# Attention over channels followed by a gated feed-forward layer: contiguous loads, scores kept in PSUM, and one written order of emission

## The chip, the cores and the metric

The kernel runs on one core of one Trainium2 chip. The metric is the device time of one execution in microseconds. Three runs of the kernel before gave 912.92, 912.98 and 914.06 us, median 912.98.

Five engines share the work, each with an instruction queue of its own that it runs in order: TensorE (PE) multiplies matrices and writes to PSUM, VectorE (DVE) and ScalarE (ACT) move and transform data, GpSimd (POOL) issues the loads that also convert f32 to bf16, and SyncE (SP) issues the stores. An engine that reaches an instruction whose inputs aren't ready waits, and everything behind it in that queue waits too.

## What is computed

```python
B, N, C = (4, 6016, 256);  d_ff = 1536
# attention over channels, for each of the 4 batches
qn = q / (norm(q, axis=1) + 1e-06)          # norms run over the 6016 rows
kn = k / (norm(k, axis=1) + 1e-06)
s  = kn.transpose(0, 2, 1) @ qn / tau       # 256 x 256 for each batch, tau = 1
a  = softmax(s, axis=-1)                    # sum + 1e-09 in the division
x  = (v @ a).reshape(24064, 256)
# gated feed-forward layer
out = (sigmoid(x @ w_gate) * (x @ w_val)) @ w_out
```

Since `x = v @ a`, both kernels form G = a @ w_gate and H = a @ w_val once for each batch (256 x 1536 each) and then compute sigmoid(v @ G) * (v @ H), so that x itself is never built. The softmax of batch b + 1 has to be complete before the first rows of that batch can go through the feed-forward part.

## The kernel before

**Tiling.** The 6016 rows of a batch are 47 tiles of 128 rows, taken in 12 groups of four (the last has three). Loads of q and k go by such groups, and the feed-forward part goes by the same groups as chunks of 512 rows (384 at the end). Row `t * 128 + p` lies on partition p, so a group is four pieces of 256 numbers on each partition.

**Attention, one group** (`attn_pair_compute`, L119). DVE squares q and k and adds the squares to running sums `acc_q` and `acc_k` (L132, L140, L146). PE multiplies k by q for the group, each half of the 256 x 256 scores in a PSUM tile of its own, `ps_sa` and `ps_sb` (L161). DVE adds both to `s_acc` in SBUF (L169, L171).

**Attention, the end** (`attn_finish`). PE sums the squares over partitions (`ps_nq`, `ps_nk`), ACT takes the roots, DVE inverts them (L193, L196) and scales the scores (L232), finds each row's maximum, ACT takes the exponential with the row sum, and DVE divides (L261). PE transposes the result (L272), and from it and the two weights makes G and H, six blocks of 512 columns each, in `ps_gh`, two matmuls a block (L292), which ACT copies to SBUF as bf16 (L299). The PSUM tiles `ps_sa`, `ps_sb`, `ps_gh`, `ps_nk`, `ps_at` and the transposes of v share two one-buffer pools, `psa` and `pst`.

**Feed-forward, one chunk** (`ffn_gv`, `ffn_out`). PE transposes the chunk of v (`ps_tp`, L322) and DVE copies it to `vT` (L328). For each of 12 blocks f of 128 hidden units PE makes `ps_gate` (L334) and `ps_val` (L343), two matmuls of 512 columns each; ACT takes the sigmoid (L351), DVE multiplies (L356) into `hT`. Two PSUM buffers each for gate and val mean that block f + 2 can't start before ACT and DVE are through with block f. Then 12 matmuls of 256 columns for each tile of rows make the output (`ps_o`, L370), which DVE copies out (L377) and SP stores.

**Order.** The code emits attention of batch 0, and then for each chunk its gate and val part, one or two groups of the next batch's attention (the next batch is spread over chunks 0 to 8, `attn_finish` in chunk 8), and the output matmuls of the chunk before. This is not the order on the engines: a scheduler reorders what is emitted, engine by engine, by priority and by what it takes to be ready. The three weights are loaded first, then q and k.

## Time and profile before

| | |
|---|---|
| median of three runs | 912.98 us |
| span of the profiled execution | 911.6 us, 14333 instructions |
| PE busy | 850.5 us, 93% |
| DVE busy | 652.5 us, 72% |
| ACT busy | 385.6 us, 42% |
| POOL busy | 110.3 us, 12% |
| loads of q, k, v and weights (q0) | 39.33 MB written, 33.1% of the 16 DMA engines |

The profile is one execution, taken by the hardware profiler. A row of its timeline reads: start in us, length in us, engine, line, operation, output and inputs, shape, count, and in brackets how long the engine had been idle before and what released it. A row of its windows reads: stretch, length, then for each engine busy time and number of instructions, then the granted PE clock, the mean number of busy DMA engines as a share of 16 (packets may overlap), and the GB/s moved as written to the destination. Matmuls are pipelined: a row's length includes the time in which the next has begun, so rates are read from the starts of rows.

### The profile page before, as it was taken

The numbers are of one execution on the slowest core, as the hardware profiler recorded it, in microseconds if no ns is written. First come the engines' busy times: TensorE is split into PE (matmuls) and PEld (weight loads), VectorE is DVE, ScalarE is ACT, GpSimd is POOL, SyncE is SP. The second block draws the span as 40 slices with busy tenths as digits, with TensorE's granted clock in tenths as the row PEclk, the third lists the DMA queues.
The fourth block names the chain that finished last, engine by engine and source line by source line (L and its number), as shares of the span: only waits on it lengthen the run. The fifth ranks groups of instructions, "written<-read, shape, count | busy, mean of one in ns | idle before, by whom it ended". The sixth has DMA issues, their size and how long they took to land.

```text
span 911.6 us, 14333 instructions
## 1 busy us (share of the span) xinstructions
PE 850.5 (93%) x5421; PEld 519.5 (57%) x5472; DVE 652.5 (72%) x1162; ACT 385.6 (42%) x660; POOL 110.3 (12%) x153
## 2 busy tenths in 40 slices
PE   1639999999899999999999999999999999999998
PEld 0324556656556565665546556656655656656566
DVE  2989976666998766766899676676747666666664
ACT  0016443345453534434563353443565344353542
POOL 5452000001510000000430000000000000000000
PEclk9999999999999999999999999999999999999999
DMA  9999211321993122113892311311122221221201
GB/s 170 196 150 176 47 37 35 63 43 38 193 144 81 19 54 52 36 36 67 127 205 45 64 36 36 68 38 36 33 58 47 54 47 36 62 44 39 52 24 65
DMA packets 101494, 64.90 MB, mean 71 GB/s; under 512 B 3120, under 2 KB 100912, under 8 KB 101424
## 3 DMA queue, kind: packets, MB, share of 16 engines
q0 software_dynamic: 76592, 39.33, 33.1%
q1 hardware_dynamic: 24832, 24.64, 8.5%
q8 instruction: 43, 0.70, 0.3%
q14 instruction: 27, 0.22, 0.1%
HBM read 78.64 MB, written 24.64 MB: 113 GB/s over the span
## 4 chain that ended last, share of the span: by engine, by line
PE 85%; DVE 6%; DMA 5%; POOL 2%; issue 1%; ACT 1%; POOLq 0%; ACTq 0%
PE ps_val L343 27%; PE ps_gate L334 26%; PE ps_o L370 24%; DMA k_full<-in_k_dram 3%; PE ps_tp L322 2%; PE ps_sb L161 2%; DVE sq L140 2%; DMA q_full<-in_q_dram 2%; PE ps_sa L161 1%; PE ps_gh L292 1%; POOL q_full L113 1%; DVE acc_q L146 1%; DVE acc_k L146 1%; DVE s_acc L171 1%; POOL k_full L117 1%
## 5 line engine op out<-in xcount | busy, mean ns | idle before, releaser
L351 ACT ACTIVATE g_sb<-ps_gate 128x512 bf16<-128x512 f32 (+1 forms) x576 | 334.9, 588 | 413.4 <-PE ps_sa L161 164.6
L356 DVE TENSOR_TENSOR hT<-ps_val,g_sb 128x512 bf16<-128x512 f32 (+1 forms) x576 | 387.6, 680 | 116.4 <-ACT g_sb L351 109.9
L343 PE MATMUL ps_val<-vT,gh_H 128*128 128x512 bf16 (+1 forms) x1150 | 336.9, 374 | 2.2
L334 PE MATMUL ps_gate<-vT,gh_G 128*128 128x512 bf16 (+1 forms) x1107 | 328.3, 375 | 5.1 <-DVE vT L328 4.6
L370 PE MATMUL ps_o<-w_out_sb,hT 128*128 128x256 bf16 x2256 | 273.4, 273 | 4.6 <-DVE out_sb L377 4.6
L370 PEld LDWEIGHTS <-hT 128*128 128x128 bf16 x2256 | 219.4, 98 | 40.7 <-issue 5.3
L343 PEld LDWEIGHTS <-gh_H 128*128 128x128 bf16 x1152 | 112.5, 98 | 128.9 <-issue 1.9
L334 PEld LDWEIGHTS <-gh_G 128*128 128x128 bf16 x1152 | 109.1, 98 | 133.9 <-DVE vT L328 10.3
L377 DVE COPY out_sb<-ps_o 128x256 f32<-128x256 f32 x188 | 79.3, 423 | 106.6 <-PE ps_o L370 105.1
L314 POOL DMA_DIRECT2D v_sb<-in_v_dram x48 | 35.8, 745 | 649.2 <-PE ps_tp L322 576.1
L161 PEld LDWEIGHTS <-k_full 128*128 128x128 bf16 x376 | 39.2, 108 | 49.8 <-DMA k_full<-in_k_dram 25.2
L161 PE MATMUL ps_sa<-q_full,k_full 128*128 128x256 bf16 x188 | 33.9, 307 | 30.3 <-DMA k_full<-in_k_dram 20.7
L113 POOL DMA_DIRECT2D q_full<-in_q_dram x48 | 36.3, 757 | 57.3 <-PE ps_sb L161 21.8
L117 POOL DMA_DIRECT2D k_full<-in_k_dram x48 | 36.5, 759 | 25.3 <-DMA k_full<-in_k_dram 21.7
L161 PE MATMUL ps_sb<-q_full,k_full 128*128 128x256 bf16 x188 | 34.4, 309 | 0.0
L328 DVE COPY vT<-ps_tp 128x1024 bf16<-128x1024 bf16 (+1 forms) x48 | 32.6, 679 | 2.5 <-PE ps_tp L322 1.8
L140 DVE TENSOR_TENSOR sq<-k_full 128x1024 bf16<-128x1024 bf16 (+1 forms) x44 | 29.7, 675 | 2.6 <-DMA k_full<-in_k_dram 2.5
L140 DVE TENSOR_TENSOR sq<-q_full 128x1024 bf16<-128x1024 bf16 (+1 forms) x44 | 29.7, 675 | 1.0 <-DMA q_full<-in_q_dram 1.0
L146 DVE TENSOR_TENSOR acc_q<-acc_q,sq 128x1024 bf16<-128x1024 bf16 (+1 forms) x44 | 29.7, 674 | 0.0
L146 DVE TENSOR_TENSOR acc_k<-acc_k,sq 128x1024 bf16<-128x1024 bf16 (+1 forms) x44 | 29.7, 674 | 0.0
L322 PE MATMUL ps_tp<-ident_bf,v_sb 128*128 128x128 bf16 x376 | 29.3, 219 | 0.1
L322 PEld LDWEIGHTS <-v_sb 128*128 128x128 bf16 x376 | 25.2, 98 | 3.2 <-issue 0.8
(48 smaller groups left out, 180.1 us busy)
## 6 DMA issues: line engine op xcount, KB each, us to landing
out_dram<-out_sb SPq DMA_DIRECT2D x44, 512.0 KB, 3.0
q_full<-in_q_dram POOLq DMA_DIRECT2D x44, 256.0 KB, 10.4
k_full<-in_k_dram POOLq DMA_DIRECT2D x44, 256.0 KB, 10.7
v_sb<-in_v_dram POOLq DMA_DIRECT2D x44, 256.0 KB, 5.2
out_dram<-out_sb SPq DMA_DIRECT2D x4, 384.0 KB, 2.6
w_gate_sb<-in_moe_w_gate_dram POOLq DMA_DIRECT2D x1, 768.0 KB, 6.7
w_val_sb<-in_moe_w_val_dram POOLq DMA_DIRECT2D x1, 768.0 KB, 9.2
w_out_sb<-in_moe_w_out_dram POOLq DMA_DIRECT2D x1, 768.0 KB, 12.5
```

The source lines that it names most:

```text
L113: nc.gpsimd.dma_start(out=st["q_full"][:, t0 : t0 + nt, :], in_=q[ab, t0 * P : (t0 + nt) * P, :].rearrange("(t p) c -> p t c", p=P),)
L117: nc.gpsimd.dma_start(out=st["k_full"][:, t0 : t0 + nt, :], in_=k[ab, t0 * P : (t0 + nt) * P, :].rearrange("(t p) c -> p t c", p=P),)
L140: nc.vector.tensor_tensor(out=sq[:, :nt, :], in0=src[:, t0 : t0 + nt, :], in1=src[:, t0 : t0 + nt, :], op=ALU.mult,)
L146: nc.vector.tensor_tensor(out=acc_t[:, :nt, :], in0=acc_t[:, :nt, :], in1=sq[:, :nt, :], op=ALU.add,)
L161: nc.tensor.matmul(ps_s, lhsT=k_full[:, t, ds(iblk * P, P)], rhs=q_full[:, t, :], start=(u == 0), stop=(u == nt - 1),)
L322: nc.tensor.transpose(out=ps_tp[:, cb, ds(u * P, P)], in_=v_sb[:, u, ds(cb * P, P)], identity=ident_bf,)
L334: nc.tensor.matmul(ps_gate[:, :nrows], lhsT=G_sb[:, ib, ds(f * P, P)], rhs=vT[:, ib, :nrows], start=(ib == 0), stop=(ib == CB - 1),)
L343: nc.tensor.matmul(ps_val[:, :nrows], lhsT=H_sb[:, ib, ds(f * P, P)], rhs=vT[:, ib, :nrows], start=(ib == 0), stop=(ib == CB - 1),)
L351: nc.scalar.activation(out=g_sb[:, :nrows], in_=ps_gate[:, :nrows], func=ACT.Sigmoid,)
L356: nc.vector.tensor_tensor(out=hT[:, f, :nrows], in0=ps_val[:, :nrows], in1=g_sb[:, :nrows], op=ALU.mult,)
L370: nc.tensor.matmul(ps_o, lhsT=hT[:, f, ds(s * P, P)], rhs=w_out_sb[:, f, :], start=(f == 0), stop=(f == FC - 1),)
L377: nc.vector.tensor_copy(out=out_sb[:, s, :], in_=ps_o)
```

## The change

The kernel is written anew around an order of emission that the engines keep: `tc.manual_schedule()` turns the reordering off.

- **Rows.** Partition p now holds rows p * 47 to p * 47 + 46 of a batch (`rows`, `out_rows`), so that a group of four tiles is one contiguous piece of 1024 numbers on each partition, in the loads and in the store. The sums over rows don't depend on which row lies where.
- **Scores.** They are kept transposed (q on the output's partitions, k along its columns), and all 47 tiles accumulate in one PSUM tile `ps_s`. `s_acc` and the DVE additions to it are gone.
- **Norms.** The norm of k is summed with a matrix of ones as before; the norm of q is made as a column, with the squares as weights and one column of ones. In batch 0 the squares go to PE group by group (`norm_mms`) and aren't added up on DVE; DVE squares q and ACT squares k. In the other batches DVE squares and adds as before.
- **Softmax.** The exponential takes a constant shift of -1 / tau in place of the row maximum, and writes bf16 in the layout that the G and H matmuls take, so the transposes are gone. Row sums are four matmuls with one column (`sums`). The division is applied where G and H are moved to SBUF (`gh`), by ACT and DVE in turn.
- **Order.** A block f of gate and val, its evictions, then four output matmuls of the chunk before, then side work out of a table (`side_work`, by slots, where slot = chunk x 12 + f): loads, score matmuls of the next batch, squares, transposes. Chunks 9 and 10 of batches 0 to 2 are "blocks": there the output matmuls stand together behind the 12 gate and val blocks, and the next batch's norms and softmax are placed in them. G and H of the next batch are made in chunk 11.
- **Loads.** All of batch 0's q and k stand ahead of the weights.

```diff
+    def rows(x, b):
+        return x[b].rearrange("(p t) c -> p t c", p=P)
+    pss = pool("pss", 1, space=PSUM)
+    psm = pool("psm", 1, space=PSUM)
+    ctx.enter_context(tc.manual_schedule())
...
+    def load_qk(b, g):
+        t0, nt = groups[g]
+        tiles = []
+        for name, src in (("q", q), ("k", k)):
+            tl = qkpool.tile([P, TPC, C], BF16, tag=name, name=name + "_sb")
+            nc.gpsimd.dma_start(out=tl[:, :nt, :], in_=rows(src, b)[:, t0 : t0 + nt, :])
+            tiles.append(tl)
+        qk[b, g] = tiles
...
+    for g in range(2):
+        load_qk(0, g)
...
+    for g in range(2, NCH):
+        load_qk(0, g)
...
+    nc.gpsimd.dma_start(out=w_gate_sb, in_=moe_w_gate.rearrange("(t p) f -> p t f", p=P))
+    load_v(0, 0)
+    nc.gpsimd.dma_start(out=w_val_sb, in_=moe_w_val.rearrange("(t p) f -> p t f", p=P))
+    load_v(0, 1)
+    nc.gpsimd.dma_start(out=w_out_sb, in_=moe_w_out.rearrange("(t p) c -> p t c", p=P))
...
+    def score(b, g, u):
+        t0, nt = groups[g]
+        q_sb, k_sb = qk[b, g]
+        if g == 0 and u == 0:
+            st[b] = {"s": pss.tile([P, CB, C], FP32, tag="s", name="ps_s")}
+        ps_s = st[b]["s"]
+        t = t0 + u
+        for j in range(CB):
+            mm(
+                ps_s[:, j, :],
+                q_sb[:, u, ds(j * P, P)],
+                k_sb[:, u, :],
+                start=(t == 0 and j == 0),
+                stop=(t == NT - 1),
+                skip_group_check=True,
+            )
...
+    def norm_mms(nq, nk, sq_q, sq_k, nt, first, last):
+        for u in range(nt):
+            mm(nk, ones_bf, sq_k[:, u, :], start=(first and u == 0), stop=(last and u == nt - 1))
+        for u in range(nt):
+            for j in range(CB):
+                mm(
+                    nq[:, j : j + 1],
+                    sq_q[:, u, ds(j * P, P)],
+                    ones_bf[:, 0:1],
+                    start=(first and u == 0 and j == 0),
+                    stop=(last and u == nt - 1),
+                    skip_group_check=True,
+                )
...
+    def norms_mm(b):
+        s = st[b]
+        nq = psm.tile([P, CB], FP32, tag="m", name="ps_nq")
+        acc_q, acc_k = s["acc"]
+        nk = pso.tile([P, C], FP32, tag="o", name="ps_nk")
+        norm_mms(nq, nk, acc_q, acc_k, TPC, True, True)
+        s["nq"], s["nk"] = nq, nk
...
+    def norms_inv(b):
+        s = st[b]
+        for r in (s["rk"], s["rq"]):
+            nc.vector.tensor_scalar(out=r, in0=r, scalar1=1e-6, scalar2=None, op0=ALU.add)
+            nc.vector.reciprocal(r, r)
...
+    def exps(b):
+        s = st[b]
+        s["e"] = attp.tile([P, CB, C], BF16, tag="e", name="e_sb", bufs=2)
+        for j in range(CB):
+            nc.scalar.activation(
+                out=s["e"][:, j, :],
+                in_=s["x"][:, j, :],
+                func=ACT.Exp,
+                bias=shift,
+                scale=s["rq"][:, j : j + 1],
+            )
...
+        ps = (pl or psm).tile([P, FG], FP32, tag=tag or "m", name="ps_gh")
+        for j in range(CB):
+            mm(
+                ps,
+                s["e"][:, j, ds(i * P, P)],
+                w_sb[:, j, ds(fg * FG, FG)],
+                start=(j == 0),
+                stop=(j == CB - 1),
+            )
+        dst = s["gh"][w][:, i, ds(fg * FG, FG)]
+        r = s["rrow"][:, i : i + 1]
+        if n % 2 == 0:
+            nc.scalar.activation(out=dst, in_=ps, func=ACT.Copy, scale=r)
+        else:
+            nc.vector.tensor_scalar(out=dst, in0=ps, scalar1=r, scalar2=None, op0=ALU.mult)
...
+    for g in range(NCH + 1):
+        if g < NCH:
+            sq[g] = (squares(0, g, 0, nc.vector), squares(0, g, 1, nc.scalar))
+            for u in range(groups[g][1]):
+                score(0, g, u)
+        if g >= 1:
+            norm_mms(nq0, nk0, *sq.pop(g - 1), groups[g - 1][1], g == 1, g == NCH)
+    st[0]["nq"], st[0]["nk"] = nq0, nk0
+    norms_sqrt(0)
+    norms_inv(0)
+    scale_k(0)
+    exps(0)
+    sums(0)
+    transpose_v(0, 0)
+    for n in range(len(gh_order)):
+        gh(0, n, *((psg, "g"), (psv, "v"))[n % 2])
...
+        for ci in range(NCH):
+            nb, nci = (b, ci + 1) if ci + 1 < NCH else (b + 1, 0)
+            lb, lci = (b, ci + 2) if ci + 2 < NCH else (b + 1, ci + 2 - NCH)
+            if nb < B:
+                at(ci * FC + 8, transpose_v, nb, nci)
+            if lb < B:
+                at(ci * FC + 0, load_v, lb, lci)
+        n = b + 1
+        if n == B:
+            return side
+        last = 9 * FC
+        for g, (t0, nt) in enumerate(groups):
+            s0 = g * last // NCH
+            at(max(0, s0 - 20), load_qk, n, g)
+            for u in range(nt):
+                at((t0 + u) * last // NT, score, n, g, u)
+            if g == 0:
+                at(0, acc_start, n)
+            for i, (fn, w) in enumerate(((acc_square, 0), (acc_add, 0), (acc_square, 1), (acc_add, 1))):
+                at(s0 + 1 + 2 * i, fn, n, g, w)
+        at(9 * FC + 10, norms_mm, n)
+        at(9 * FC + 11, norms_sqrt, n)
+        at(10 * FC + 1, norms_inv, n)
+        at(10 * FC + 4, scale_k, n)
+        at(10 * FC + 11, exps, n)
+        at(11 * FC + 0, sums, n)
+        for i in range(len(gh_order)):
+            at(11 * FC + i, gh, n, i)
...
+        side = side_work(b)
+        for ci in range(NCH):
+            block = b + 1 < B and ci in (9, 10)
+            for f in range(FC):
+                glu(b, ci, f)
+                flush()
+                if prev is not None and not block:
+                    out_mms(*prev, f * TPC, (f + 1) * TPC)
+                for fn, a in side.get((ci, f), ()):
+                    fn(*a)
+            if prev is not None and block:
+                for s in range(TPC):
+                    out_mms(*prev, s * FC, (s + 1) * FC)
+                    flush()
+            prev = (b, ci)
```

The order of the instructions shows the change at three places.

The first is POOL's queue at the start of the program, where the loads are issued; before, it begins so, with the identity matrix, the three weights, and then q and k in groups:

```order
masks.py:197 MEMSET ident_bf 128x128
L82 DMA w_gate_sb<-in_moe_w_gate_dram 128x2x1536
masks.py:199 ISA
masks.py:199 AFFINE_SELECT ident_bf<-ident_bf 128x128
L86 DMA w_val_sb<-in_moe_w_val_dram 128x2x1536
L90 DMA w_out_sb<-in_moe_w_out_dram 128x12x256
L113 DMA q_full<-in_q_dram 128x4x256
L117 DMA k_full<-in_k_dram 128x4x256
```

Of the change, POOL's queue from the last loads of batch 0's q and k (the two of 768 columns) to the first ones of batch 1:

```order
L95 DMA q_sb<-in_q_dram 128x768
L95 DMA k_sb<-in_k_dram 128x768
L123 DMA w_gate_sb<-in_moe_w_gate_dram 128x2x1536
L104 DMA v_sb<-in_v_dram 128x1024
L125 DMA w_val_sb<-in_moe_w_val_dram 128x2x1536
L104 DMA v_sb<-in_v_dram 128x1024
L127 DMA w_out_sb<-in_moe_w_out_dram 128x12x256
L104 DMA v_sb<-in_v_dram 128x1024
L95 DMA q_sb<-in_q_dram 128x1024
L95 DMA k_sb<-in_k_dram 128x1024
```

The weights moved from ahead of batch 0's 24 loads of q and k to behind them, with three loads of v among and behind them, and batch 1's first q and k stand behind all of these.

The second place is PE's queue where the feed-forward part of batch 0 begins. Before, the first gate matmuls stand behind score matmuls of batch 1:

```order
L161 LDWEIGHTS k_full
L161 MATMUL ps_sa<-q_full,k_full 128x256
L334 LDWEIGHTS gh_G
L334 MATMUL ps_gate<-vT,gh_G 128x512
L334 LDWEIGHTS gh_G
L334 MATMUL ps_gate<-vT,gh_G 128x512
L343 LDWEIGHTS gh_H
L343 MATMUL ps_val<-vT,gh_H 128x512
```

Of the change, the end of the first block (f = 0) of batch 0's first chunk, and the start of the second; all matmuls have the line of a helper, and `ps_s` are batch 1's scores:

```order
L85 LDWEIGHTS gh_H
L85 MATMUL ps_val<-vT,gh_H 128x512
L85 LDWEIGHTS q_sb
L85 MATMUL ps_s<-k_sb,q_sb 128x256
L85 LDWEIGHTS q_sb
L85 MATMUL ps_s<-k_sb,q_sb 128x256
L85 LDWEIGHTS gh_G
L85 MATMUL ps_gate<-vT,gh_G 128x512
```

The score matmuls now come one tile at a time between the blocks of gate and val, the first of them behind the very first block, and the second block stands behind them.

The third place is DVE's queue where the next batch's norms are inverted, in chunk 8 before and in chunk 10 now. Before:

```order
L356 TENSOR_TENSOR hT<-ps_val,g_sb 128x512 x12
L171 TENSOR_TENSOR s_acc<-s_acc,ps_sb 128x256
L377 COPY out_sb<-ps_o 128x256
L193 TENSOR_SCALAR hq_rep<-hq_rep 128x256
L196 RECIPROCAL hq_rep<-hq_rep 128x256
L220 TENSOR_SCALAR gk<-ps_kc 128x2
L232 TENSOR_TENSOR x_sb<-s_acc,hq_rep 128x256
```

Of the change:

```order
L352 COPY out_sb<-ps_o 128x256 x4
L326 TENSOR_TENSOR hT<-ps_val,g_sb 128x512 x2
L216 TENSOR_SCALAR rk<-rk 128x256
L217 RECIPROCAL rk<-rk 128x256
L216 TENSOR_SCALAR rq<-rq 128x2
L217 RECIPROCAL rq<-rq 128x2
L326 TENSOR_TENSOR hT<-ps_val,g_sb 128x512 x3
L227 TENSOR_TENSOR x_sb<-ps_s,rk 128x256 x2
L326 TENSOR_TENSOR hT<-ps_val,g_sb 128x512 x4
```

The inversion stood behind all twelve products `hT` of a chunk, among the copies of finished output; it now stands between the second and the third product of a chunk, and the scaling of the scores between the fifth and the sixth.

More of the change, by code (lines that the diff above doesn't have):

```diff
@@ L2 @@
-import math
 from contextlib import ExitStack
@@ L321, in ffn_gv, with transpose_v @@
+    vts = {}
+    def transpose_v(b, ci):
+        t0, nt = groups[ci]
+        v_sb = vs.pop((b, ci))
+        ps_tp = psm.tile([P, CB, CH], BF16, tag="m", name="ps_tp")
+        for u in range(nt):
             for cb in range(CB):
```

483 lines of the change are left out of this document (161 added, 322 removed).

## The prediction

> **What bounds the kernel now.** First the page: span, share of PE, the span in 40 slices, the chain that ended last.
>
> ```profile
> span 911.6 us, 14333 instructions
> PE 850.5 (93%) x5421; PEld 519.5 (57%) x5472; DVE 652.5 (72%) x1162; ACT 385.6 (42%) x660; POOL 110.3 (12%) x153
> PE   1639999999899999999999999999999999999998
> PEclk9999999999999999999999999999999999999999
> PE 85%; DVE 6%; DMA 5%; POOL 2%; issue 1%; ACT 1%; POOLq 0%; ACTq 0%
> ```
>
> A slice is 22.8 us. PE is full from the fifth on, and nearly idle in the first three. So there are two questions: how soon PE can begin, and how close to its own work it runs afterwards. For the second, PE's rates from its timeline and the chain:
>
> ```profile
> 643.49 0.59 PE L334 MATMUL ps_gate<-vT,gh_G 128*128 128x512 bf16 x2
> 650.39 0.59 PE L334 MATMUL ps_gate<-vT,gh_G 128*128 128x512 bf16 x2
> 120.81 4.80 PE ps_o L370 x44
> 245.20 0.61 PE L322 MATMUL ps_tp<-ident_bf,v_sb 128*128 128x128 bf16 x8
> 245.65 0.60 PE L161 MATMUL ps_sa<-q_full,k_full 128*128 128x256 bf16 x4
> 80.12 0.59 PE L334 MATMUL ps_gate<-vT,gh_G 128*128 128x512 bf16 x2 [0.32 <-DVE vT L328]
> 899.04 8.42 PE ps_o L370 x77
> ```
>
> Eight blocks (two gate and two val matmuls each) take 650.39 - 643.49 = 6.90 us, so 0.2156 a matmul of 512 columns; 44 output matmuls of 256 columns take 4.80, so 0.1091; eight transposes take 0.45, so 0.056. For 384 columns I take three quarters of 512, 0.162. The feed-forward part begins at 80.1 and PE ends at 899.04 + 8.42 = 907.5; the last copy, store and landing end the span 4.1 later. Work between, in these rates: gate and val 4 x (11 x 48 x 0.2156 + 48 x 0.162) = 486.4; output 188 x 12 x 0.1091 = 246.1; transposes 20.7; scores of three batches 282 x 0.1091 = 30.8, less 0.9 that was done by 80.1; G and H of three batches 72 x 0.2156 = 15.5; norms, transposes and columns in `attn_finish` about 4.6. Sum 803. The stretch is 827.4, so **24 us are waits**, 8 in each of the first three batches. Some are seen:
>
> ```profile
> 231.50 2.78 PE L370 MATMUL ps_o<-w_out_sb,hT 128*128 128x256 bf16 x24 [1.56 <-DVE out_sb L377]
> 247.48 0.38 PE L334 MATMUL ps_gate<-vT,gh_G 128*128 128x512 bf16 x1 [1.24 <-DVE vT L328]
> 777.77 0.74 POOL L314 DMA_DIRECT2D v_sb<-in_v_dram  x1 [15.39 <-PE ps_tp L322]
> 793.90 0.74 POOL L314 DMA_DIRECT2D v_sb<-in_v_dram  x1 [15.39 <-PE ps_tp L322]
> ```
>
> In the last batch, which has no side work, a chunk takes 16.13 (793.90 - 777.77) for 48 x 0.2156 + 48 x 0.1091 + 0.45 = 16.03 of work: 0.1 of wait a chunk. There is little to win there.
>
> For the first question, the start:
>
> ```profile
> 0.00:4.00 4.00, 0.00 (x0) 0.00 (x0) 0.17 (x2) 1.28 (x1) 3.04 (x9) 1.00 0.29 28
> 4.00:8.00 4.00, 0.00 (x0) 0.00 (x0) 0.00 (x0) 0.00 (x0) 3.93 (x6) 1.00 1.06 204
> 24.00:28.00 4.00, 3.25 (x16) 1.86 (x14) 4.00 (x9) 0.00 (x0) 2.20 (x3) 1.00 1.45 196
> 48.00:52.00 4.00, 2.79 (x14) 1.82 (x13) 4.00 (x10) 0.00 (x0) 0.00 (x0) 1.00 0.95 131
> 1.28 0.85 POOL L82 DMA_DIRECT2D w_gate_sb<-in_moe_w_gate_dram  x1 [0.33 <-issue]
> 18.39 1.03 PE L161 MATMUL ps_sa<-q_full,k_full 128*128 128x256 bf16 x4 [18.39 <-DMA k_full<-in_k_dram]
> 47.78 1.01 PE L161 MATMUL ps_sa<-q_full,k_full 128*128 128x256 bf16 x4 [1.21 <-DVE s_acc L171]
> 58.99 0.69 DVE L132 TENSOR_TENSOR acc_k<-k_full 128x1024 bf16<-128x1024 bf16 x1 [0.44 <-DMA k_full<-in_k_dram]
> 59.60 1.75 DVE L196 RECIPROCAL hq_rep<-hq_rep 128x256 f32<-128x256 f32 x1
> 69.57 4.69 PE L292 MATMUL ps_gh<-w_gate_sb,aT_sb 128*128 128x512 bf16 x11 [0.92 <-DVE aT_sb L278]
> ```
>
> The weights come first and fill the path (204 GB/s), so the first scores wait until 18.4. Then DVE, full in the two later windows, paces the groups by four squares and sums and two additions to `s_acc`. After the last group DVE, in order, stands before batch 1's squares, whose loads land at 58.99, and only then inverts batch 0's norms. G and H begin at 69.6 and the feed-forward part at 80.1.
>
> **The change, part by part.**
>
> *The start: loads.* Ahead of batch 1's first q and k, POOL now issues 24 loads of q and k (6016 KB as bf16), the weights (2304) and three of v (768); with that pair (512) 9600 KB, 9.83 MB. PE must have this pair behind the first gate and val block, since its score matmuls stand there.
>
> ```profile
> q_full<-in_q_dram POOLq DMA_DIRECT2D x44, 256.0 KB, 10.4
> L356 DVE TENSOR_TENSOR hT<-ps_val,g_sb 128x512 bf16<-128x512 f32 (+1 forms) x576 | 387.6, 680 | 116.4 <-ACT g_sb L351 109.9
> L140 DVE TENSOR_TENSOR sq<-k_full 128x1024 bf16<-128x1024 bf16 (+1 forms) x44 | 29.7, 675 | 2.6 <-DMA k_full<-in_k_dram 2.5
> ```
>
> The rate of 2 KB pieces isn't in the trace; q and k in 512 B pieces ran at 196, w_gate in 3 KB pieces at 204, so the ends are 50.2 and 48.2 us and I take 0.2 MB/us, 49.2. Issue starts at 0.74 instead of 1.28; data flowed about 1.3 behind the end of the first issue (112 KB by 4.0), so from 2.8. Landing is seen about 0.8 behind the data (first scores at 18.39; the weights and one pair, 2816 KB, are through by 17.6 at these rates). So the pair lands at 2.8 + 49.2 + 0.8 = **52.8**, between 51.8 and 53.8.
>
> *The start: the chain.* All of q and k is through at 2.8 + 6.16/0.2 = 33.6, landed 34.4. Behind it: ACT's square 0.9, scores and norm matmuls of the last two groups 1.7, root 0.6 with its table loaded before, inversion 2.4, scaling 0.8, exponentials 1.2, sums and their inverse 0.9, transposes 0.5, twelve G and H blocks 5.2 at full rate: 48.6 (root, inversion and scaling by the rows quoted under the waits; the square, exponentials and sums are estimates from ACT's 0.60 there). The eleven gh matmuls of the row above took 4.69, 0.427 each, twice the 0.2156, though the granted clock reads full all through: after a stretch with hardly any matmul PE ran at half rate. The chain idles PE about 5 us, so I add 2.4, half of a 4.7 us stretch: 51. The first block then ends near 51.9, before the pair lands. So the load sets the start, and half rate costs nothing as long as it stays below 1 us more. The Trainium skill, "TensorE: Matmul & The Clock Gate", Part 1, says that PE's clock is gated to half after an idle window of about 3.4 us and freed after about as long a busy one; these rows agree. By its figure the addition would be an estimated 1.7 instead of 2.4. By that rule PE could also stay at half rate among the gaps of the load stage; that is a rival below.
>
> *The steady part.* Its work is the same to within 1 us: norms and sums 1.1 a batch instead of 1.5, no transposes of the softmax; the 36 row sums and norm columns with one moving column aren't in the trace, between 0 and the 0.1091 of 256 columns, taken as a transpose's 0.056. So 803, of which the first block (0.86) is done at 52.8. DVE's work, now without `s_acc`, lies beside PE: per slot 0.68 for hT, 0.30 for squares and sums (four of 0.675 in nine slots), 0.2 for copies, 1.2 against PE's 0.86 + 0.44 + 0.09 = 1.4; without that cover each slot of the first nine chunks would be DVE's. ACT's `Square` and DVE's scaled eviction of gh, new, lie beside a 2.6 us load per group and a 1.5 us slot; if that cover went, the second's 0.7 would show 18 times, 12 us.
>
> *Waits that the written order adds, a batch (batches 0 to 2).*
>
> ```profile
> 227.07 0.51 DVE L193 TENSOR_SCALAR hq_rep<-hq_rep 128x256 f32<-128x256 f32 x1
> 227.61 1.75 DVE L196 RECIPROCAL hq_rep<-hq_rep 128x256 f32<-128x256 f32 x1
> 229.40 0.42 DVE L232 TENSOR_TENSOR x_sb<-s_acc,hq_rep 128x256 f32<-128x256 f32 x1
> 651.02 0.60 ACT L351 ACTIVATE g_sb<-ps_gate 128x512 bf16<-128x512 f32 x1 [0.27 <-PE ps_gate L334]
> 651.64 1.28 ACT L192 ACT_TABLE_LOAD   x1
> 652.93 0.38 ACT L192 ACTIVATE hq_rep<-ps_nq 128x256 f32<-128x256 f32 x1
> 651.25 0.49 PE L161 MATMUL ps_sb<-q_full,k_full 128*128 128x256 bf16 x3
> ```
>
> Chunk 10: the inversion (227.07 to 229.40 and a second small one, 2.4) stands ahead of the third product hT. Behind it wait PE's val blocks, two buffers deep and 0.86 apart; DVE's slack of 0.18 a block covers little: 2.2 of wait. Chunk 9: in these rows the root ends 2.06 behind the end of PE's val matmuls (653.31 against 651.25, where PE turns to scores), and the second output tile needs its buffer 1.31 behind: 0.8. Chunk 11: the only buffer of `psm` passes from the row sums over DVE to the first gh block, 0.45, and from the transposes over `vT` (0.68) to the ninth, 0.8. Together 4.2, three times 12.6. With 0.1 a chunk (4.7) **17 us**, bounded by 0 and by twice the three-batch part, 30.
>
> *The sum.* 52.8 + 803 - 0.9 + 17 + 4.1 = 876 of span. The median stands 1.4 above the span of the profiled run (912.98 against 911.6): **877.5**, 35 less: 28 from the start, 7 from fewer waits.
>
> **The rivals.**
>
> *Fewer waits.* The written order hides most of them, as the scheduler did before with others: 17 falls to about 6, 866. For it: the last batch's chunks lie within 1% of their work. Against: PE's queue holds nothing behind the inversion that could go first.
>
> *PE at half rate in the load stage.* In 18.39's row four score matmuls take 1.03, half rate by 0.2 each. A group would need twelve of these and eight small ones up to 0.1: 3.2 against 2.6 of loading. Twelve groups end near 45, the chain adds 14, the first block ends near 60, 7 behind the pair: 884.5. Against: a PE that has fallen behind has no gaps left, and the gh matmuls, without gaps, were followed by full rate at 80.12.
>
> *Waits twice as long*, from DVE falling behind in chunks 9 to 11: 890.
>
> *An exposed weight load: slower than before.* Output matmuls now alternate with gate and val in 41 chunks x 12 = 492 slots. If one weight load a slot lies open,
>
> ```profile
> L370 PEld LDWEIGHTS <-hT 128*128 128x128 bf16 x2256 | 219.4, 98 | 40.7 <-issue 5.3
> 252.09 0.81 PE L334 MATMUL ps_gate<-vT,gh_G 128*128 128x512 bf16 x3
> 252.74 0.38 PE L370 MATMUL ps_o<-w_out_sb,hT 128*128 128x256 bf16 x2
> 252.96 0.59 PE L343 MATMUL ps_val<-vT,gh_H 128*128 128x512 bf16 x2
> ```
>
> 98 ns x 492 = 48 us, 926; it decides from 72 ns a slot. Against: where the scheduler mixed them, three gates took 0.65 and two outputs 0.22, full rate.
>
> *The change doesn't do what it says:* 2 KB pieces run no faster than 196. That moves the pair by 1 us only; the gain at the start comes from order.
>
> **How the numbers follow.** Forecast 877.5 (871 to 884) 0.60; fewer waits 0.13; half rate 0.11; double waits 0.09; weight loads or a stall of that size 0.06; a tie 0.01. The range 865 to 892 takes in all but the last two. Faster by over 0.2% (about what a measurement of this kernel tells from no change) 0.93, within 0.2% 0.01, slower 0.06.
>
> **What would show it.** The second gate block at 52 to 54 us, released by the load of k; PE waits of about 2 us in chunk 10 on hT, 0.8 in chunk 9 on ps_o; mid-batch chunks of 16.1 us plus scores; 4 us behind the last matmul. Wrong would be: gh after 53, idle PE in every slot, or DVE busy throughout chunks 0 to 8.

## The result and the profile after

The changed kernel takes 874.56 us (median of four runs, 873.64 to 876.81) against 913.16 of the kernel before (912.92 to 914.06). The ratio is 0.958, 95% interval 0.9565 to 0.9594: faster. The profiled execution took 875.38 with a span of 873.3.

From the page of the changed kernel, the lines that answer to those of before:

```profile
span 873.3 us, 14462 instructions
PE 837.9 (96%) x5601; PEld 526.3 (60%) x5601; DVE 600.7 (69%) x1020; ACT 392.6 (45%) x644; POOL 79.7 (9%) x153
PE   5599999999999999999899999999989999999998
PEclk9889999999999999999999999999999999999999
PE 89%; DMA 5%; DVE 3%; ACT 1%; issue 1%; POOL 0%; ACTq 0%; POOLq 0%
```

PE is full from the third slice of 21.8 us on, not from the fifth of 22.8. Two slices of the granted clock read 8 now: the profile shows a PE that isn't at full speed. Two later slices show an 8 for PE, the twentieth and the thirtieth: the ends of batches 1 and 2.

The start, from PE's timeline of the changed kernel (start, length, instructions, and in brackets the idle time and its releaser), and two windows of it (the last three numbers: granted clock, DMA share, GB/s):

```profile
6.54 1.86 PE L85 MATMUL ps_s<-k_sb,q_sb 128*128 128x256 bf16 x8 [6.54 <-DMA k_sb<-in_k_dram]
14.62 1.03 PE L85 MATMUL ps_s<-k_sb,q_sb 128*128 128x256 bf16 x8
34.35 0.82 PE L85 MATMUL ps_s<-k_sb,q_sb 128*128 128x256 bf16 x6 [0.27 <-DMA k_sb<-in_k_dram]
48.84 0.59 PE L85 MATMUL ps_gate<-vT,gh_G 128*128 128x512 bf16 x2
51.98 0.58 PE L85 MATMUL ps_s<-k_sb,q_sb 128*128 128x256 bf16 x2 [2.11 <-DMA k_sb<-in_k_dram]
52.35 1.06 PE L85 MATMUL ps_gate<-vT,gh_G 128*128 128x512 bf16 x2
55.59 0.38 PE L85 MATMUL ps_s<-k_sb,q_sb 128*128 128x256 bf16 x2
...
24.00:28.00 4.00, 2.45 (x35) 2.12 (x33) 1.38 (x2) 1.56 (x2) 2.03 (x4) 1.00 1.12 208
52.00:56.00 4.00, 4.00 (x13) 1.68 (x13) 1.43 (x3) 1.19 (x2) 1.06 (x2) 0.58 1.12 209
```

The first scores come at 6.5 instead of 18.4, at half rate (eight in 1.86, and 1.03 from 14.62 on; the granted clock reads 1.00 all the while), the last group at 34.35, the first gate block at 48.84. Then PE waits 2.11 for batch 1's k. The eight matmuls behind it take until 55.59, 0.41 each and not 0.2156: half rate. The feed-forward part began at 80.1 before; here it is as if it had begun some 27 us sooner.

The end of a batch, from the view of PE's waits (total, times, longest) and from PE's timeline, with the first transposes of chunk 1 in batches 1 and 2 as marks:

```profile
PE ps_val L85 <- DVE hT L326: 4.9, 3, 1.6
PE ps_gh L85 <- DVE vT L301: 2.3, 3, 0.8
PE ps_o L85 <- ACT rq L211: 1.3, 2, 0.6
PE ps_gh L85 <- DVE rrow L257: 1.2, 3, 0.4
...
270.96 0.61 PE L295 MATMUL ps_tp<-ident_bf,v_sb 128*128 128x128 bf16 x8
480.49 0.61 PE L295 MATMUL ps_tp<-ident_bf,v_sb 128*128 128x128 bf16 x8
```

A batch takes 480.49 - 270.96 = 209.53. Its work, in the prediction's rates, is 121.6 for gate and val, 61.5 output, 5.2 transposes, 10.3 scores, 5.2 G and H, 1.1 norms and sums: 204.9. So 4.6 a batch are left as waits. In the last batch the loads of v stand 16.05 apart (752.93 - 736.88 below) for 16.03 of work, and PE's last matmuls end at 869.7, 3.6 ahead of the span's end:

```profile
736.88 0.53 POOL L104 DMA_DIRECT2D v_sb<-in_v_dram  x1 [15.52 <-PE ps_tp L295]
752.93 0.53 POOL L104 DMA_DIRECT2D v_sb<-in_v_dram  x1 [15.52 <-PE ps_tp L295]
865.14 4.53 PE L85 MATMUL ps_o<-w_out_sb,hT 128*128 128x256 bf16 x40
```

### The profile page after: what moved, and what is told of

Its sections match the earlier page's. It is cut to its first block, busy times and chain, and to the rows that moved or that the text cites. A ratio compares the mean times of both kernels' runs of the same rounds, so it can differ in the third digit from the quotient of the medians.

```text
span 873.3 us, 14462 instructions
## 1 busy us (share of the span) xinstructions
PE 837.9 (96%) x5601; PEld 526.3 (60%) x5601; DVE 600.7 (69%) x1020; ACT 392.6 (45%) x644; POOL 79.7 (9%) x153
## 4 chain that ended last, share of the span: by engine, by line
PE 89%; DMA 5%; DVE 3%; ACT 1%; issue 1%; POOL 0%; ACTq 0%; POOLq 0%
PE ps_o L85 27%; PE ps_gate L85 27%; PE ps_val L85 27%; DMA k_sb<-in_k_dram 5%; PE ps_s L85 4%; PE ps_tp L295 2%; PE ps_gh L85 2%; DVE hT L326 1%; ACT g_sb L325 1%; DVE rk L217 1%; ACT L210 0%; DVE out_sb L352 0%; DVE vT L301 0%; DVE gh_H L284 0%; DVE gh_G L284 0%
## 5 line engine op out<-in xcount | busy, mean ns | idle before, releaser
L85 PE MATMUL ps_o<-w_out_sb,hT 128*128 128x256 bf16 x2256 | 326.7, 273 | 1.9 <-ACT rq L211 1.3
L85 PE MATMUL ps_s<-k_sb,q_sb 128*128 128x256 bf16 x376 | 68.7, 282 | 15.9 <-DMA k_sb<-in_k_dram 15.9
L85 PEld LDWEIGHTS <-q_sb 128*128 128x128 bf16 x376 | 37.1, 100 | 23.8 <-issue 10.6
L156 DVE TENSOR_TENSOR sq<-q_sb 128x1024 bf16<-128x1024 bf16 (+1 forms) x45 | 30.2, 672 | 25.5 <-PE ps_nq L85 19.4
L194 DVE TENSOR_TENSOR acc<-acc,sq 128x1024 bf16<-128x1024 bf16 (+1 forms) x66 | 44.2, 669 | 0.0
L95 POOL DMA_DIRECT2D q_sb<-in_q_dram x48 | 26.3, 548 | 19.5 <-PE ps_gh L85 6.7
L95 POOL DMA_DIRECT2D k_sb<-in_k_dram x48 | 26.4, 550 | 9.5 <-DMA k_sb<-in_k_dram 6.1
L156 DVE TENSOR_TENSOR sq<-k_sb 128x1024 bf16<-128x1024 bf16 (+1 forms) x33 | 22.1, 669 | 0.0
L154 ACT ACTIVATE sq<-k_sb 128x1024 bf16<-128x1024 bf16 (+1 forms) x12 | 12.5, 1039 | 20.8 <-DMA k_sb<-in_k_dram 17.3
L85 PEld LDWEIGHTS <-e_sb 128*128 128x128 bf16 x112 | 10.5, 102 | 14.8 <-issue 7.9
```

Of the source, the lines that this page charges most:

```text
L85: nc.tensor.matmul(out, lhsT=lhsT, rhs=rhs, start=start, stop=stop, **kw)
L95: nc.gpsimd.dma_start(out=tl[:, :nt, :], in_=rows(src, b)[:, t0 : t0 + nt, :])
L154: nc.scalar.activation(out=sq[:, :nt, :], in_=src[:, :nt, :], func=ACT.Square)
L156: engine.tensor_tensor(out=sq[:, :nt, :], in0=src[:, :nt, :], in1=src[:, :nt, :], op=ALU.mult)
L194: nc.vector.tensor_tensor(out=acc[:, :nt, :], in0=acc[:, :nt, :], in1=st[b]["sq", w][:, :nt, :], op=ALU.add)
```

## The experiments

| kernel | median, us | ratio to before (95%) | profiled span |
|---|---|---|---|
| the change | 874.56 | 0.958 (0.9565 to 0.9594) | 873.3 |
| a_rows: rows as before | 879.57 | 0.9622 (0.9595 to 0.9649) | 877.3 |
| a_wfirst: weights first | 884.62 | 0.9676 (0.9653 to 0.9699) | 881.8 |
| a_sqfirst: batch 1's squares first | 888.19 | 0.972 (0.9704 to 0.9736) | 886.0 |
| b_qkfirst: before, q and k first | 909.25 | 0.9944 (0.9921 to 0.9966) | 907.7 |
| a_noil: blocks in every chunk | 888.56 | 0.9717 (0.9695 to 0.9739) | 885.4 |
| a_mix11: mixed in chunk 11 alone | 874.21 | 0.9571 (0.9555 to 0.9587) | 872.3 |
| a_noblk: no blocks | 888.48 | 0.9727 (0.9713 to 0.9741) | 886.4 |
| a_pair: pair early | 872.64 | 0.9553 (0.9539 to 0.9567) | 870.3 |
| a_inv: inversion in a block | 868.79 | 0.9518 (0.95 to 0.9535) | 869.7 |
| a_buf: two PSUM conflicts gone | 865.32 | 0.9475 (0.9461 to 0.9488) | 863.0 |
| a_best: the last three together | 858.84 | 0.9397 (0.9382 to 0.9413) | 857.0 |
| a_best_all: and PE, ACT kept ready | 856.40 | 0.9371 (0.9356 to 0.9386) | 854.2 |

### What the start is made of

Four kernels undo, or do alone, one part of the change each. Rows:

```diff
-        return x[b].rearrange("(p t) c -> p t c", p=P)
+        return x[b].rearrange("(t p) c -> p t c", p=P)
-    out_rows = out.rearrange("(b p t) c -> b p t c", b=B, p=P)
+    out_rows = out.rearrange("(b t p) c -> b p t c", b=B, p=P)
```

> The changed kernel with the old assignment of rows to partitions (row t x 128 + p on partition p, for loads and stores), all else as changed. Theory (contiguous pieces only raise the load rate, and the load of batch 1's first pair sets the start): q, k and v in 512 B pieces at the 196 GB/s of the kernel before, the weights at 204, so 7.47 MB / 0.196 + 2.36 MB / 0.204 = 49.7 us of data instead of 9.83 MB / 0.2085 = 47.1; the second gate block moves from 52 to about 54.6, POOL's issues go back from 0.55 to 0.74 us, nothing else changes: 2.6 us slower, about 877. Rival one (contiguity is a large part of the gain, through the stores and the later loads): 8 us or more slower, with waits on loads or stores in mid-batch. Rival two (no effect): within 0.5 us, second block still at 52.

The second block waits for k until 55.94 instead of 51.98, and the span is 4.0 longer, not 2.6. PE's waits for other engines are the same to 0.2 us, so the theory's place was right and its rate was not: the first scores come 0.5 later (7.05), and the windows from 4 to 12 us run at 178 and 176 GB/s, which is 0.8 more; only later ones run at 196.

```profile
4.00:8.00 4.00, 0.95 (x5) 0.81 (x6) 0.69 (x1) 0.97 (x1) 3.92 (x8) 1.00 1.36 178
55.94 0.59 PE L85 MATMUL ps_s<-k_sb,q_sb 128*128 128x256 bf16 x2 [2.41 <-DMA k_sb<-in_k_dram]
```

The loads of the weights, moved:

```diff
...
+    nc.gpsimd.dma_start(out=w_gate_sb, in_=moe_w_gate.rearrange("(t p) f -> p t f", p=P))
+    nc.gpsimd.dma_start(out=w_val_sb, in_=moe_w_val.rearrange("(t p) f -> p t f", p=P))
+    nc.gpsimd.dma_start(out=w_out_sb, in_=moe_w_out.rearrange("(t p) c -> p t c", p=P))
     for g in range(2):
         load_qk(0, g)
...
-    nc.gpsimd.dma_start(out=w_gate_sb, in_=moe_w_gate.rearrange("(t p) f -> p t f", p=P))
     load_v(0, 0)
-    nc.gpsimd.dma_start(out=w_val_sb, in_=moe_w_val.rearrange("(t p) f -> p t f", p=P))
     load_v(0, 1)
-    nc.gpsimd.dma_start(out=w_out_sb, in_=moe_w_out.rearrange("(t p) c -> p t c", p=P))
```

> The changed kernel with the three weights loaded ahead of batch 0's q and k. Theory (batch 0's chain is only 3 us short of the load, so that 2.36 MB / 0.208 = 11.3 us ahead of it make the chain the bound): batch 0's last scores at 45.7 instead of 34.35, first gate block at 60.1 instead of 48.84, second at 61; the wait for the load of k (2.1) and the half rate behind it (1.8) go: 9.0 - 1.8 = 7.2 us slower, about 882. Rival (the load of batch 1's first pair alone sets the start, and it lands at 52 in any order): no change.

PE's timeline:

```profile
46.22 0.82 PE L85 MATMUL ps_s<-k_sb,q_sb 128*128 128x256 bf16 x6 [0.33 <-DMA k_sb<-in_k_dram]
60.50 0.59 PE L85 MATMUL ps_gate<-vT,gh_G 128*128 128x512 bf16 x2
62.92 0.59 PE L85 MATMUL ps_gate<-vT,gh_G 128*128 128x512 bf16 x2 [0.31 <-ACT g_sb L324]
```

No wait for k; the chain is the bound. The span is 8.5 longer, not 7.2: the first block comes 0.4 later than expected, and in the third PE waits for `g_sb`, a wait that the pair's had covered.

DVE's old order:

```diff
+    load_v(0, 2)
+    load_qk(1, 0)
+    st[1] = {}
+    acc_start(1)
+    acc_square(1, 0, 0)
+    acc_square(1, 0, 1)
     norms_inv(0)
...
```

The side work leaves these five out in their old places.

> The changed kernel with DVE's old order at the end of batch 0's attention: batch 1's first squares of q and k stand ahead of the inversion of batch 0's norms; loads as in the changed kernel. Theory (in the kernel before this order, not the order of loads, set when the feed-forward part began): DVE waits for the pair that lands near 52, the inversion begins at about 52.7 instead of 36.8, the first gate block at 64.7 instead of 48.84, with no wait for k and no half rate behind it: 11 us slower than the changed kernel, about 886. Rival (the order of loads alone, which here is the new one, makes the start): within 3 us of the changed kernel.

From DVE's timeline and PE's:

```profile
50.75 0.69 DVE L185 TENSOR_TENSOR acc<-q_sb 128x1024 bf16<-128x1024 bf16 x1 [16.06 <-DMA q_sb<-in_q_dram]
52.91 1.75 DVE L217 RECIPROCAL rk<-rk 128x256 f32<-128x256 f32 x1
55.90 0.18 PE L85 MATMUL ps_r<-ones_bf,e_sb 128*128 128x1 bf16 x1 [19.62 <-ACT e_sb L235]
```

DVE waits 16 us for data that nobody on the path needs yet, and the span is 12.7 longer. This is the largest of the three parts, with all loads in their new order. In the kernel before itself the waits at this place were 3.93 and 0.44, since there DVE came to them only at 53.7.

The other way round, the kernel before with its three weights loaded behind batch 0's q and k:

```diff
-    w_gate_sb = wpool.tile([P, CB, DFF], BF16)
-    nc.gpsimd.dma_start(
-        out=w_gate_sb, in_=moe_w_gate.rearrange("(t p) f -> p t f", p=P)
-    )
...
     for pi in range(n_pairs):
         attn_dma_pair(0, pi)
         attn_pair_compute(0, pi)
+    w_gate_sb = wpool.tile([P, CB, DFF], BF16)
+    nc.gpsimd.dma_start(
+        out=w_gate_sb, in_=moe_w_gate.rearrange("(t p) f -> p t f", p=P)
+    )
...
     attn_finish(0)
```

> The kernel before with one part of the change alone: batch 0's q and k are issued ahead of the three weights. DVE's order stays as it was: batch 1's first squares stand ahead of the inversion of batch 0's norms. Theory (in the kernel before DVE's order, not the order of loads, held the start): the first scores come at 7 instead of 18.4 and the last group some 11 us sooner, but DVE then stands before batch 1's squares, whose loads still land near 58, since the bytes ahead of them are the same; inversion at 59 to 60, feed-forward part at 80, 913 as before. Rival (the order of loads is the gain): 11 us faster, 902, with the inversion near 48.

In between: 3.9 of span. DVE's timeline of this kernel, and POOL's timeline of the kernel before and of this one:

```profile
53.57 0.69 DVE L119 TENSOR_TENSOR acc_q<-q_full 128x1024 bf16<-128x1024 bf16 x1 [10.18 <-DMA q_full<-in_q_dram]
55.52 1.75 DVE L183 RECIPROCAL hq_rep<-hq_rep 128x256 f32<-128x256 f32 x1
```

```profile
53.23 0.75 POOL L113 DMA_DIRECT2D q_full<-in_q_dram  x1 [11.17 <-DVE acc_k L146]
```

```profile
42.95 0.75 POOL L100 DMA_DIRECT2D q_full<-in_q_dram  x1 [7.10 <-DVE acc_k L133]
```

The mechanism is the theory's, but not its size: DVE is through with batch 0's scores 10.2 us sooner, and gives 6.1 of that up, since its waits ahead of the inversion grow from 3.93 and 0.44 to 10.18 and 0.25. The inversion comes 4.1 sooner. Its reason for the landing at 58 was wrong. In the kernel before, the load of batch 1's q wasn't held by the bytes ahead of it: each of q and k has one buffer for a whole batch, and the trace has the issue at 53.23 released by DVE's last addition of squares of batch 0. With q and k first the buffer is free at 43, and the bytes ahead hold it until 53.57. The kernel before thus had a loop: DVE frees the buffer, the buffer lets the load start, and DVE waits for that load ahead of work that needs nothing of it.

So the parts don't add up, each being the bound once the others are gone: undone singly, contiguity costs 4, load order 8.5, DVE's order 12.7.

Two more parts of the start were not undone by any run; the traces give only their place. With the weights first in both, batch 0's last scores begin at 46.22 in `a_wfirst` and at 50.85 in the kernel before, where DVE's additions pace the groups: 4.6 sooner, in which the faster loads have a share. And from the start of the reciprocal to the first gate block the kernel before takes 80.12 - 59.60 = 20.5, the change 48.84 - 37.32 = 11.5: 9.0 less for a softmax without maximum, division and transposes, and for G and H moved by two engines.

### Mixed output matmuls and blocks

```diff
-            block = b + 1 < B and ci in (9, 10)
+            block = True
```

> The changed kernel with the output matmuls of every chunk in one block behind the twelve gate and val blocks (as chunks 9 and 10 have it), none between the blocks. Theory (the interleaving hides DVE's side work, and costs PE nothing): the last batch keeps its 16.05 us a chunk, and chunks 0 to 8 of batches 0 to 2 become DVE's: 0.68 for hT, 0.30 for squares and sums, 0.06 for vT is 1.04 a slot against PE's 0.86 + 0.10 of scores + 0.04 of transposes = 1.00: 0.04 x 12 x 27 = 13 us slower, between 0 and 30, with PE waiting on hT for ps_val. Rival (an exposed weight load in the mixed slots): faster, with the last batch's chunks below 16.05.

The total fits, the reason doesn't. The first transposes of chunks 3 and 4 stand 17.35 apart here and 17.36 in the change:

```profile
88.75 0.61 PE L295 MATMUL ps_tp<-ident_bf,v_sb 128*128 128x128 bf16 x8
106.10 0.61 PE L295 MATMUL ps_tp<-ident_bf,v_sb 128*128 128x128 bf16 x8
...
PE ps_gh L85 <- DVE gh_G L284: 3.5, 9, 0.4
PE ps_gh L85 <- DVE rrow L257: 2.5, 3, 0.8
```

DVE keeps up in chunks 0 to 8 (the expectation took 0.68 for a product, an instruction's length; back to back they stand 0.60 apart). The rival falls too: in the last batch the same transposes stand 16.04 apart (727.94 - 711.90), and 16.05 in the change with its mixed output matmuls (735.97 - 719.92). By the waits the loss is in chunk 11, where each block of G and H waits for the one PSUM buffer. That was a reading after the fact, so a kernel tests it:

```diff
-            block = b + 1 < B and ci in (9, 10)
+            block = ci != NCH - 1
```

> The changed kernel with the output matmuls in one block in all chunks but the last one of a batch (chunk 11), where they are mixed in four by four as in the change. In the run with blocks everywhere chunks 1 to 8 took 17.14 us as in the changed kernel, and PE waited in chunk 11 for evictions of G and H. Theory (mixing is worth something only where G and H are evicted from one PSUM buffer; elsewhere DVE keeps up without it, at its back-to-back pace of 0.60 for hT): 874 within 1.5 us, chunks 1 to 8 at 17.14, PE's waits as in the changed kernel. Rival (mixing hides DVE's work in chunks 0 to 8 too, and the 14 us of that run come from there): 880 or more.

874.21: mixing is worth something in chunk 11 alone, about 14 us in three batches. No blocks at all:

```diff
-            block = b + 1 < B and ci in (9, 10)
+            block = False
```

> The changed kernel with the output matmuls of chunks 9 and 10 of batches 0 to 2 also mixed in four by four, no blocks. Theory (the inversion of 2.4 us makes PE wait in chunk 10 because gate and val blocks there follow each other every 0.86 us; with the output matmuls between them a slot is 1.3 and two buffers cover 2.6): PE's waits on hT for ps_val fall from 4.9 us to below 1, those on rq and rk for ps_o from 1.9 to about 1.3 (the buffer that ps_nk takes is wanted a little later): 3 to 5 us faster, about 870.5. Rival (the blocks are what keeps the norms' root and inversion off PE's path): 2 to 6 us slower, with new waits on ACT's table loads or on copies of out_sb in chunks 9 and 10.

Both theories miss. The wait on hT shrinks only to 4.0, and new ones come in chunk 11. PE's timeline and a window behind them:

```profile
237.65 0.18 PE L85 MATMUL ps_r<-ones_bf,e_sb 128*128 128x1 bf16 x1 [0.65 <-ACT e_sb L235]
240.93 1.01 PE L85 MATMUL ps_gh<-w_gate_sb,e_sb 128*128 128x512 bf16 x2 [2.56 <-DVE rrow L257]
240.00:244.00 4.00, 3.08 (x11) 1.56 (x11) 1.60 (x5) 1.18 (x2) 0.00 (x0) 0.50 1.14 191
```

The block of chunk 10, 48 output matmuls or 5.2 us, stands between the exponentials and the row sums. It hides two table loads of ACT and the exponentials. Without it PE waits 0.65 and 0.31 for the exponentials; the second table load then holds up the sigmoid, and DVE's step behind the row sums stands behind the product that needs it: 2.56. The granted clock reads 0.50 from 239.25 to 246.1, so PE's work behind these waits runs at half rate for some 5 us. A batch (same marks) takes 215.16 instead of 209.53. By these waits it is the block of chunk 10 that is needed; no run takes chunk 9's away alone.

### The waits that the written order left

The pair early:

```diff
     nc.gpsimd.dma_start(out=w_val_sb, in_=moe_w_val.rearrange("(t p) f -> p t f", p=P))
+    load_qk(1, 0)
     load_v(0, 1)
...
-            at(max(0, s0 - 20), load_qk, n, g)
+            if (n, g) != (1, 0):
+                at(max(0, s0 - 20), load_qk, n, g)
```

> The changed kernel with batch 1's first q and k issued ahead of v's second chunk and of w_out, which is wanted a chunk later. Theory (the load of that pair sets the start, and the wait for it drops PE to half rate): the pair lands near 46, the wait of 2.11 at 51.98 goes and the second block comes at about 49.9; the half rate from 52 to 55.6 goes too, 1.8: 3.9 us faster, about 870.7. Rival one (half rate is not a consequence of that wait but follows the chain's idle time anyway): the second block at 49.9, but half rate for 3 us behind it, 2.1 us faster. Rival two (the next load, group 1 or w_out, is late instead): a wait of 2 us in the first or second chunk, no gain.

```profile
50.09 0.59 PE L85 MATMUL ps_gate<-vT,gh_G 128*128 128x512 bf16 x2
51.42 0.59 PE L85 MATMUL ps_gate<-vT,gh_G 128*128 128x512 bf16 x2 [0.31 <-ACT g_sb L326]
```

The second block starts at 50.09, without half rate: rival one fell. The span is 3.0 shorter, not 3.9: a wait on `g_sb` (0.31, ACT's table for the sigmoid) appears, and the first block comes 0.17 later. The median is only 1.9 lower, for a reason that the section on the hardware gives.

The inversion, and the two conflicts:

```diff
-        at(10 * FC + 1, norms_inv, n)
...
                     out_mms(*prev, s * FC, (s + 1) * FC)
                     flush()
+                    if ci == 9 and s == 1:
+                        norms_inv(b + 1)
```

> The changed kernel with the inversion of the norms (2.4 us of DVE) moved from behind the second product of chunk 10 into the block of output matmuls of chunk 9, behind the copy of its second tile, where DVE has only copies to do. Theory (it makes PE wait for hT three times 1.64 us): those waits go, nothing takes their place, since the third and fourth copy are wanted only a chunk later: 4.9 us faster, about 869.7. Rival (the copies of chunk 9's third and fourth tile now hold the output buffers): a wait on out_sb of about 1.5 us a batch takes its place, and the gain is below 1 us.

```diff
-        nq = psm.tile([P, CB], FP32, tag="m", name="ps_nq")
+        nqk = psm.tile([P, CB + C], FP32, tag="m", name="ps_nq")
+        nq, nk = nqk[:, 0:CB], nqk[:, CB : CB + C]
...
-        nk = pso.tile([P, C], FP32, tag="o", name="ps_nk")
...
-            at(11 * FC + i, gh, n, i)
+            at(11 * FC + i, gh, n, i, *((pss, "s"), (psm, "m"))[i % 2])
```

> The changed kernel with two PSUM conflicts taken away: the norm of k is summed into the same tile of the one-buffer pool as the norm of q, so that it takes no buffer of the output tiles, and the G and H blocks of chunk 11 alternate between that pool and the score tile's, which is free there. Theory (the waits are for buffers): PE's waits on rq and rk for ps_o (1.9 us in all), on vT for ps_gh (2.3) and on rrow for ps_gh (1.2) go: 5.4 us faster, about 869.2. Rival (they are waits for the data that moves, and return a block later): less than 2 us faster, with waits of the same length on another tile in chunks 9 and 11.

Both theories held in what they named, though the second gained 9.2 us (865.32) where it expected 5.4. A batch takes 207.86 with the first (1.67 less) and 206.66 with the second:

```profile
266.31 0.61 PE L296 MATMUL ps_tp<-ident_bf,v_sb 128*128 128x128 bf16 x8
472.97 0.61 PE L296 MATMUL ps_tp<-ident_bf,v_sb 128*128 128x128 bf16 x8
```

That is 2.87 less a batch, where the view of the waits had shown 1.8. The view counts idle time from the modelled end of the last matmul: a row of two matmuls of 512 columns is 0.59 long, though the next may begin 0.43 behind its start. So each of these nine waits costs about 0.16 more than it reads, 0.5 a batch, and a short one isn't listed: in chunk 11 of the change four output matmuls of 0.44 began at 244.91 and the next block of G and H only at 245.65. The spans differ by 10.3: 8.6 in the three batches, and 1.7 by a start that in this run was without half rate.

All three together, and then two additions at the start:

> The changed kernel with the early pair, the inversion in the block of chunk 9 and the two PSUM conflicts taken away, all three at once. Theory (the gains are of different waits and add up): from the run with the conflicts taken away (span 863.0, its start without half rate) 5.0 less for the inversion (1.67 us a batch as measured) and 1.6 for the pair: span 856.4, median about 858.5; PE's waits in chunks 9 to 11 gone. Rival (a wait taken away lets the next one show): 861 or more, with new waits in chunks 9 to 11 or in the first chunk.

```diff
+    warm = psg.tile([P, FG], FP32, tag="g", name="ps_warm")
+    for i in range(34):
+        mm(warm[:, :C], ident_bf, qk[0, NCH - 1][1][:, 0, :], True, True)
     norms_inv(0)
     scale_k(0)
     exps(0)
+    pre = attp.tile([P, 1], FP32, tag="pre", name="pre")
+    nc.scalar.activation(out=pre, in_=shift, func=ACT.Sigmoid)
```

> The kernel of the run before, and two additions at the start: 34 matmuls of 256 columns into a PSUM tile that nothing reads, put on PE while DVE inverts and scales batch 0's norms, and a sigmoid of one column on ACT behind the exponentials, so that its table is loaded during G and H. Theory (G and H of batch 0 run at half rate because PE was idle some 4 us before, and the first gate blocks wait for ACT's table): transposes and the 24 G and H matmuls at 42 to 48.8 run at full rate from the start, 5.2 instead of 6.7 us, and the 0.31 wait on g_sb goes: 1.5 to 2.5 us faster than the run before, about 856.5. Rival (PE isn't what paces this stretch; the evictions of G and H by ACT and DVE or the load of the next group are): within 0.7 us of it.

The gains add up: 858.84. PE's timeline of `a_best`, the same marks, and of `a_best_all`, the start:

```profile
263.68 0.61 PE L297 MATMUL ps_tp<-ident_bf,v_sb 128*128 128x128 bf16 x8
468.68 0.61 PE L297 MATMUL ps_tp<-ident_bf,v_sb 128*128 128x128 bf16 x8
```

```profile
36.00 3.87 PE L85 MATMUL ps_warm<-k_sb,ident_bf 128*128 128x256 bf16 x34
41.60 1.03 PE L85 MATMUL ps_gh<-w_gate_sb,e_sb 128*128 128x512 bf16 x3
46.37 1.03 PE L85 MATMUL ps_gh<-w_val_sb,e_sb 128*128 128x512 bf16 x4
```

A batch takes 205.00 for 204.9 of work by the prediction's rates: hardly anything is left in it. With PE kept busy through the softmax of batch 0, G and H run at full rate (20 matmuls in 46.37 - 41.60, the record of one missing, with a wait of 0.29 on `w_val`) and the granted clock stays at 1.00: 2.8 less of span, 2.4 less in the median. The two additions were made together; by the traces the first gate block comes 2.05 sooner (47.23 for 49.28), and the rest is the wait on `g_sb`, which is gone. 856.40 is the fastest version here, 6.3% under the kernel before (6.1 to 6.4 by the interval).

## Why the prediction was right

877.5 was predicted, 874.56 came. By its steps, against the profiled execution:

- **What sets the start.** Right: the second gate block waits for the load of batch 1's k, at 51.98 where 52.8 stood. With the other parts undone the bound moved to the chain, where the run's expectation had it (60.50 for 60.1 with the weights first).
- **"Half rate costs nothing as long as it stays below 1 us more."** Half right. In the chain it cost nothing: the first block ended 2.1 ahead of the pair. But the wait for the pair, which the prediction itself had put there, dropped PE to half rate again, 1.7 us that no term held. The rival of half rate in the load stage fell: PE ran slowly until 14.6, fell behind, had no gaps from 9.11 on, and came to full rate.
- **Waits of the written order.** 4.2 a batch, 12.6 in all, were predicted, each on its engine; 4.53 a batch came off when they were undone (205.00 against 209.53), 13.6 in all. Singly: the inversion 1.67 where 2.2 stood, the conflicts of root, row sums and `vT` together 2.87 where 2.05 stood.
- **The 0.1 a chunk, 4.7.** The one term that was wrong in size: 0.02 a chunk, 1 us. It was taken over from the kernel before, whose scheduled order it belonged to.
- **The tail.** 3.6 where 4.1 stood.
- **"28 from the start, 7 from fewer waits."** About 27 and 11 of the 38.3 by which the spans differ; the waits gave more because of the 4.7.
- **Exposed weight loads** didn't show: 16.05 a chunk with mixed output matmuls. **DVE's cover**, which the prediction held necessary for the first nine chunks, wasn't: with blocks everywhere these took as long. It was worked out from lengths of instructions instead of their spacing.
- **"The gain at the start comes from order."** Right between the parts that were undone, but contiguous pieces gave 4, not 1: 2 KB pieces ran at 208 where 200 was taken, and in 512 B pieces the first windows are slower than 196. The softmax that is 9.0 shorter isn't order, and no run undid it.

The sum: 0.8 less at the start, 1.0 more for waits, 1.7 for half rate, 3.7 less in the chunks, 0.5 less at the end: 876 - 2.3 = 873.7 for a span of 873.3. That the total came so close is partly luck: 2.7 us that the prediction didn't have, most of it half rate, are hidden by the 3.7 that it had too many.

## What to carry to other kernels

Look at what an in-order engine has queued ahead of the work on the path: with the new load order, 16 us of DVE waiting for early squares cost 12.7, more than the 8.5 of the old load order. When an order is written out, its remaining waits can be read off one by one and undone, here down to 205.0 us a batch for 204.9 of work. A filler on one engine (the block of output matmuls in chunk 10) may be the only cover of a chain on two others, so ask for each block what runs beside it.

## What the runs showed of the hardware

Whether a short wait brings half rate depends on when it falls. Quarter-microsecond windows of the changed kernel:

```profile
38.25:38.50 0.25, 0.00 (x0) 0.00 (x0) 0.25 (x1) 0.07 (x1) 0.00 (x0) 0.65 1.08 213
45.00:45.25 0.25, 0.25 (x2) 0.08 (x1) 0.00 (x0) 0.25 (x1) 0.25 (x1) 0.69 1.46 199
51.75:52.00 0.25, 0.03 (x1) 0.02 (x1) 0.18 (x1) 0.00 (x0) 0.00 (x0) 0.96 1.12 205
55.25:55.50 0.25, 0.25 (x2) 0.13 (x1) 0.25 (x1) 0.25 (x1) 0.00 (x0) 0.72 1.11 205
```

If the clock is 1.0 or 0.5, these put the drops at 38.33 and 51.98 and the rises at 45.15 and 55.39: 6.83, 6.83 and 3.41 apart, so steps of 3.41. (Before 38 the marks don't serve: the granted clock reads 1.00 from 8 to 12 us, where eight score matmuls took 1.87.) In the stretch that ended at 51.98 PE was busy from 48.57 to 49.86, 1.3 us, and lost its clock all the same. In `a_buf` the steps lay elsewhere (drop at 38.78, rise at 45.61), PE waited 1.92 instead of 2.11, and stayed at full rate:

```profile
51.87 0.38 PE L85 MATMUL ps_s<-k_sb,q_sb 128*128 128x256 bf16 x2 [1.92 <-DMA k_sb<-in_k_dram]
52.09 0.59 PE L85 MATMUL ps_gate<-vT,gh_G 128*128 128x512 bf16 x2
```

Nor is it the length: `a_noblk` and `a_noil` waited 2.39 and 2.35 there and stayed at full rate. The Trainium skill, "TensorE: Matmul & The Clock Gate", Part 1, has a window of 3413 ns that runs freely; the trace agrees with that, but here a stretch with 1.3 us of work counted as idle. Counted on in steps of 3.41 from the last rise, the step that holds the wait for the pair had this much PE work (lengths of rows, so with modelled ends):

| run | wait for the pair, us | PE busy in the step, us | clock behind it |
|---|---|---|---|
| the change | 2.11 | 1.30 | half |
| a_rows | 2.41 | 1.33 | half |
| a_inv | 2.01 | 1.41 | half |
| a_buf | 1.92 | 1.49 | full |
| a_noil | 2.35 | 1.52 | full |
| a_noblk | 2.39 | 1.58 | full |
| a_mix11 | 1.59 | 1.82 | full |

The work in the step sorts the runs, the wait doesn't: in these seven executions the line lies between 1.41 and 1.49 us of 3.41. No run was made to find it. The likely mark of the half rate in the times: the spans of the change were 871.9, 872.0, 873.3 and 875.0, and those of `a_inv` 866.7 to 867.1 and once, in the profiled run with half rate, 869.7. With the pair early, which takes the wait away, they lay within 0.9.

A matmul with one moving column takes about 0.03, not the 0.056 that the prediction took: in `a_wfirst` eight of them stand ahead of the next at 47.51.

```profile
47.30 0.34 PE L85 MATMUL ps_nq<-ones_bf,sq 128*128 128x1 bf16 x8
47.51 0.49 PE L85 MATMUL ps_nk<-sq,ones_bf 128*128 128x256 bf16 x3
```

POOL's issue of a load of q or k takes 0.53 us with contiguous pieces and 0.74 in `a_rows` without, besides the rate (208 GB/s instead of 196).
